# Five edits to a fused transform, mixing and two-layer kernel: where the first narrowing, an addition, a weight split, the threshold input and one transform stage stand

## The chip, the cores and the metric

The kernel runs on one core of a Trainium2 chip. A core has a matrix engine (TensorE, in the profile PE, with its weight loads as PEld), a vector engine (VectorE, DVE), an activation engine (ScalarE, ACT), a general engine (GpSimd, POOL) and a queue engine that issues DMAs (SyncE, SP; ACT issues the stores here). Each engine runs its own instructions in order. They meet through semaphores. The metric is the device time of one execution in microseconds (us), as the median of several runs.

## The reference, cut to what matters

The input `x` is 8 sequences of 3008 rows of 256 channels, all float32; the four matrices of the second part come in float64.

```
X = rfft(x, axis=1)                      # along the 3008 rows
Yr = Xr @ w_r - Xi @ w_i + b_r           # mixing over channels
Yi = Xr @ w_i + Xi @ w_r + b_i
Y = sign(Y) * max(|Y| - 0.01, 0)         # threshold, on both parts
a = irfft(Y, n=3008)
h = relu(a^T @ w_tok1) @ w_tok2          # over the rows (tokens), 256 wide
u = a + h^T
out = u + relu(u @ w_ch1) @ w_ch2        # over the channels, 1536 wide
```

## The kernel before

**Transform.** 3008 is 47 times 64. The forward transform is a 47-point stage (`dft47`, 13 groups of 5 positions; `stage1` multiplies a group by the constant `f1` and stores the result `a` to HBM as `a_d`), then a 64-point stage (`forward`: PSUM tile `px`, one step for each of 12 pairs `kp`). The inverse is again 64 points (`inverse`, tile `pi`, stored as `b_d`) and 47 points, the last one fused into the sum that makes `u` (`make_u`, tile `pu`, L738).

**Mixing and threshold.** `forward` copies `px` into `xf` as real and imaginary part (ACT, L442) and adds the two (L443), because the complex product is done with three real ones. `mix` runs three products into PSUM banks `p1` and `p2` (tile `pm`), adds the bias and the partial sums on DVE (L469 to L471), and thresholds the result. For the non-plain units the 32-bit operands are split into a high and a low part in the format fp32r (`split`, L137 on ACT for the high part, L140 for the low part), and each product is three matmuls (`mm3`, L178 to L180).

**Units.** The batch is worked in five units: sequence 0, sequence 1, and three pairs. Unit 0 is "plain" (unsplit float32 matmuls) and is done ahead of everything by `begin`; its 47-point result stays on the chip as `z`, is turned by PE (`turn`, tile `pz`) and copied to `a2` (tile `a`; the first two by DVE at L428, the others by ACT at L430).

**Work that `begin` carries as well.** The float64 matrices arrive as raw 64-bit words (`load_raw`) and are narrowed to float32 by two ACT and six DVE instructions (`narrow`, L151 to L158; tile `wide`). The 13 groups of `w_tok1` are narrowed and sent through the same 47-point stage (`prepare_w1`, tile `p`, L246 and L247, stored as `a_w`), read back (`load_w`, L319) and transformed over 64 points (`make_w`, tile `pw`, L327). `begin` loops over `n` from 0 to 21: `forward(n)`, `mix(n-1)`, one or two groups of `w_tok1`, `inverse(n-3)`; from n = NW = 10 on `make_w` and `tokens` (tile `gp`, L507). `prepare_mix` makes the sums of the mixing weights (L361 to L363), and `split_mix` splits them for the later units into `wmh` and `wml`, at n = 10.

**Main loop.** `channel(n)` does the two-layer part on up to 512 tokens (tiles `ph`, L178 to L180, and `po`; ACT L776 and DVE L777 between). Between its steps the loop at the end of the kernel runs the generator `spectral(u + 1)` of the next unit: each step yields an estimated cost, and a step runs while `left_s > pace * left_c`, that is, spread evenly over what is left of the present unit. A step that yields "wait" holds the generator until `left_c` has dropped by 10 more:

```
            if hold is not None:
                if left_c > hold:
                    continue
                pace, hold = left_s / left_c, None
```

**What sets the order.** The source is not the order of execution. The framework lays out each engine's instructions ahead of the run: it goes through the program with its own cost estimates, and gives an engine the earliest instruction of the source that it believes to be ready then. On the chip that order is kept, and an instruction whose data are late holds up all that are behind it on its engine. Transfers start when their buffer is free: five raw buffers, three `ld` tiles, two `ev` tiles (the `a` of `stage1`).

Lines that the prediction refers to: L137 and L140 (`split`), L151 to L158 (`narrow`), L167 (raw loads), L226 and L227 (`sum_diff`), L246 to L250 (`stage1`), L319, L327, L330 (`w_tok1`), L428 and L430, L440 to L443, L464 to L475 (`mix`).

Of the kernel before, what the change touches and what calls it, by code (L numbers as in the profile page):

```python
# [121 lines left out]
def tile_kernel(ctx: ExitStack, tc: tile.TileContext, io):  # L122
# [46 lines left out]

    def load_wide(src, n, pool=None, tag="o", raw=None):  # L170
        if raw is None:
            raw = load_raw(src, n, pool)
        rows = raw.shape[0]
        tmp = wk.tile([rows, 2, n], F32, tag=tag, name="wide", bufs={"o": 3, "hl": 4}[tag])
        return narrow(raw, tmp[:, 0], tmp[:, 1])

# [87 lines left out]

    def dft47(load, dst, w, ahead, eng, pool=None, turned=False):
        xs = [load(g) for g in range(ahead)]
        yield 0.0
        sds = {}

        def prepare(g):  # L270
            if g < NG:
                sds[g] = sum_diff(xs[g], g, w, eng, pool)
                xs[g] = None

        def divide(g):
            if g < NG and pool is None:
                sds[g] = split_x(sds[g], w)

        prepare(0)
        prepare(1)  # L280
        divide(0)
        for g in range(NG):
            if g + ahead < NG:
                xs.append(load(g + ahead))
            prepare(g + 2)
            divide(g + 1)
            if turned:
                stage1_turned(sds.pop(g), dst, g)
            else:
                stage1(sds.pop(g), dst, g, w, pool)  # L290
            yield 0.7 * w / C
# [12 lines left out]

    def prepare_w1(pool):
        def load(g):
            f = load_wide(None, 2 * DT, pool, ("hl", "o")[g % 7 % 2], raw=raws.pop(g)).rearrange("p (i w) -> p i w", i=2)
            load_raw1()
            return f

        return dft47(load, a_w, DT, 3, None, pool)
# [38 lines left out]
    def load_mix():  # L350
        wf = wc["wf2"] = const.tile([128, 2, 2, C], F32, tag="gl", name="wf2")
        for i, name in enumerate(("w_r", "w_i")):
            DMA.dma_start(out=wf[:, i], in_=io[name].rearrange("(t p) c -> p t c", p=128))
        load_raw1()
        for i, name in enumerate(("b_r", "b_i")):
            DMA.dma_start(out=bias[:, i], in_=io[name].rearrange("(o c) -> o c", o=1).to_broadcast([128, C]))
# [9 lines left out]

    def split_mix(y):
        for i, w in enumerate(wc["mix"]):
            V.tensor_copy(out=wmh[:1, i, 0, :1], in_=y[:1, 0, :1])
            split(wmh[:, i], wml[:, i], w, S, V)  # L370
# [21 lines left out]
    def parts(u):  # L392
# [40 lines left out]
        def forward(kp, b, a2):  # L433
            pt = bank("px")
            for t in range(2):
                for ab in range(2):
                    o = (2 * t + ab) * 128
                    cs = slice(t * 128, (t + 1) * 128)
                    x = a2[:, ab, b, cs]
                    PE.matmul(pt[:, o:o + 128], lhsT=x, rhs=f2cols(2 * kp + ab), start=True, stop=True)  # L440
            xf = wk.tile([128, 3, 4, 64], F32, tag="xth" if plain else "xf", name="xf", bufs=2)
            S.copy(out=xf[:, 1:3], in_=pt.rearrange("p (q i m) -> p i q m", i=2, m=64))  # L442
            (V if plain else G).tensor_tensor(out=xf[:, 0], in0=xf[:, 1], in1=xf[:, 2], op=ALU.add)  # L443
            if plain:
                return xf
            xh = wk.tile([128, 3, 2, 128], F32R, name="xth", bufs=2)
            xl = wk.tile([128, 3, 2, 128], F32R, name="xtl", bufs=2)
            fl = "p i (t a) m -> p i t (a m)"
            split(xh, xl, xf.rearrange(fl, t=2), S, V)
            return xh, xl  # L450

        def mix(kp, xt, yh, yl):
# [3 lines left out]
            else:  # L456
                p1, p2 = bank("pm1"), bank("pm2")
            for j, out in ((0, p1[:, :C]), (2, p2[:, C:]), (1, p2[:, :C])):

# [9 lines left out]
            V.tensor_tensor(out=y, in0=p1[:, :C].rearrange("p (o c) -> p o c", o=1).to_broadcast([128, 2, C]), in1=bias, op=ALU.add)  # L469
            V.tensor_tensor(out=y[:, 0], in0=p2[:, C:], in1=y[:, 0], op=ALU.add)  # L470
            V.tensor_tensor(out=y[:, 1], in0=p2[:, :C], in1=y[:, 1], op=ALU.add)  # L471
            if plain:
# [49 lines left out]
    def spectral(u):  # L522
        p = parts(u)
        nb = p.nb
        yield from dft47(p.load_unit, p.a, p.w, 3, V if u == 1 else G)
        yield "wait"
# [43 lines left out]
    def begin(sp):  # L570
# [14 lines left out]
        with tc.tile_pool(name="early", bufs=1) as early:  # L585
# [9 lines left out]
            load_mix()  # L595
            for _ in range(4):
                load_raw1()
# [3 lines left out]
            prepare_mix()  # L601
            w1 = prepare_w1(early)
            a2s = {0: p.turn(0), 1: p.turn(1)}
            next(w1)
            es, xts = {k: load_e(k) for k in range(2)}, {}
# [5 lines left out]
            for n in range(NW + KP):  # L611
                if n == NW:
                    split_mix(ys[NW - 2])
                if n < KP:
# [220 lines left out]
    for n, (u, at, cw) in enumerate(chunks):  # L835
# [8 lines left out]
        for c in channel(n):  # L844
# [9 lines left out]
            while left_s > pace * left_c:  # L854
                step = next(sp, None)
                if step is None:
                    left_s = -1e9
                elif step == "wait":
                    hold = left_c - 10.0
                    break  # L860
# [38 lines left out]
```

## Time and profile before

| | us |
|---|---|
| median of 3 runs | 2448.39 (2446.65 to 2452.34) |
| the profiled execution, own time | 2449.02 |
| its span, first to last instruction | 2447.0 |
| PE busy | 2423.0 (99% of the span) |
| DVE busy | 1109.7 (45%) |
| ACT busy | 876.4 (36%) |
| POOL busy | 305.7 (12%) |
| PE idle before its first matmul | 6.6 |
| last PE matmul to the end of the span | 4.3 |
| mean granted clock of TensorE | 0.998 |

Busy time is the time in which an engine executes instructions, the span the time from the first to the last instruction. The idle time of an engine stands with the engine whose result ended it. The granted clock is a share of full speed; here it takes one of two values, 1.00 or 0.50. The span less PE's busy time is 24.0 us, and 10.9 us of that are the start and the end of the program.

### The profile page before, as it was taken

The numbers are of one execution on the slowest core, as the hardware profiler recorded it, in microseconds if no ns is written. First come the engines' busy times: TensorE is split into PE (matmuls) and PEld (weight loads), VectorE is DVE, ScalarE is ACT, GpSimd is POOL, SyncE is SP. The second block draws the span as 40 slices with busy tenths as digits, with TensorE's granted clock in tenths as the row PEclk, the third lists the DMA queues.
The fourth block names the chain that finished last, engine by engine and source line by source line (L and its number), as shares of the span: only waits on it lengthen the run. The fifth ranks groups of instructions, "written<-read, shape, count | busy, mean of one in ns | idle before, by whom it ended". The sixth has DMA issues, their size and how long they took to land.

```text
span 2447.0 us, 31693 instructions
## 1 busy us (share of the span) xinstructions
PE 2423.0 (99%) x12848; PEld 2115.4 (86%) x12848; DVE 1109.7 (45%) x1774; ACT 876.4 (36%) x1580; POOL 305.7 (12%) x259
## 2 busy tenths in 40 slices
PE   8999999999999999999999999999999999999999
PEld 7778999988888888888888888888888888888887
DVE  7986655454455444433344363434334333232332
ACT  6764444443333343333333353333333222222222
POOL 0000222212223011111111120111111000000000
PEclk9999999999999999999999999999999999999999
DMA  7864335543324352222322263232321212112110
GB/s 206 254 211 144 101 115 154 162 142 99 94 84 129 107 176 79 61 80 87 93 75 68 89 182 100 77 99 76 93 67 37 70 50 63 56 52 81 37 56 18
DMA packets 144239, 246.07 MB, mean 101 GB/s; under 512 B 10653, under 2 KB 97917, under 8 KB 144093
## 3 DMA queue, kind: packets, MB, share of 16 engines
q1 hardware_dynamic: 114313, 190.56, 26.2%
q10 hardware_dynamic: 29780, 53.49, 7.0%
q8 instruction: 101, 1.65, 0.3%
q14 instruction: 45, 0.37, 0.0%
HBM read 159.73 MB, written 84.28 MB: 100 GB/s over the span
## 4 chain that ended last, share of the span: by engine, by line
PE 94%; DVE 2%; DMA 2%; ACT 1%; SPq 1%; issue 0%; POOL 0%; DVEq 0%; ACTq 0%; POOLq 0%
PE ph L178 10%; PE ph L179 10%; PE ph L180 10%; PE po L178 10%; PE po L180 10%; PE po L179 10%; PE pu L738 5%; PE px L440 3%; PE pm L178 2%; PE pm L180 2%; PE pm L179 2%; PE pu L178 2%; PE pu L179 2%; PE pu L180 2%; PE gp L178 2%; PE gp L179 2%
## 5 line engine op out<-in xcount | busy, mean ns | idle before, releaser
L777 DVE SCALAR_TENSOR_TENSOR hlo<-ph,hh 128x512 fp32r<-128x512 f32 (+4 forms) x588 | 391.9, 667 | 639.1 <-ACT hh L776 636.2
L776 ACT ACTIVATE hh<-ph 128x512 fp32r<-128x512 f32 (+4 forms) x588 | 340.7, 580 | 818.7 <-PE ph L180 816.6
L178 PE MATMUL ph<-uh,w 128*128 128x512 f32 (+4 forms) x1176 | 455.9, 388 | 1.0 <-DVE hlo L777 1.0
L179 PE MATMUL ph<-ul,w 128*128 128x512 f32 (+4 forms) x1176 | 449.6, 382 | 0.0
L178 PE MATMUL po<-hh,w2h 128*128 128x512 f32 (+4 forms) x1176 | 449.0, 382 | 0.0
L180 PE MATMUL ph<-uh,w 128*128 128x512 f32 (+4 forms) x1176 | 448.8, 382 | 0.0
L179 PE MATMUL po<-hlo,w2h 128*128 128x512 f32 (+4 forms) x1176 | 448.2, 381 | 0.0
L180 PE MATMUL po<-hh,w2l 128*128 128x512 f32 (+4 forms) x1176 | 448.1, 381 | 0.0
L180 PEld LDWEIGHTS ph<-uh,w 128*128 128x128 f32 x1176 | 221.1, 188 | 39.6
L179 PEld LDWEIGHTS po<-hlo,w2h 128*128 128x128 f32 x1176 | 221.1, 188 | 38.6 <-DVE hlo L777 0.2
L180 PEld LDWEIGHTS po<-hh,w2l 128*128 128x128 f32 x1176 | 221.0, 188 | 38.7
L178 PEld LDWEIGHTS po<-hh,w2h 128*128 128x128 f32 x1176 | 221.1, 188 | 38.6
L178 PEld LDWEIGHTS ph<-uh,w 128*128 128x128 f32 x1176 | 221.4, 188 | 36.3 <-DVE hlo L777 1.9
L179 PEld LDWEIGHTS ph<-ul,w 128*128 128x128 f32 x1176 | 221.5, 188 | 34.0 <-DVE ul L747 0.2
L140 DVE TENSOR_TENSOR xtl<-xf,xth 128x768 fp32r<-128x768 f32 x84 | 80.5, 959 | 207.3 <-ACT xth L137 207.3
L178 PE MATMUL pm<-wmh,xth 128*128 128x256 f32 x504 | 144.4, 287 | 1.1 <-ACT xth L137 1.1
L140 POOL TENSOR_TENSOR yl<-z,yh 128x512 fp32r<-128x512 f32 x72 | 92.8, 1289 | 412.8 <-ACT yh L137 412.8
L745 ACT COPY uf<-pu 128x470 f32<-128x470 f32 (+23 forms) x188 | 62.7, 376 | 227.5 <-PE pu L738 227.5
L180 PE MATMUL pm<-wmh,xtl 128*128 128x256 f32 x504 | 142.4, 283 | 0.0
L179 PE MATMUL pm<-wml,xth 128*128 128x256 f32 x504 | 142.4, 283 | 0.0
L738 PEld LDWEIGHTS pu<-g,b 96*128 96x128 f32 x1024 | 130.8, 191 | 3.4
L443 POOL TENSOR_TENSOR xf<-xf 128x256 f32<-128x256 f32 x84 | 69.2, 824 | 482.7 <-ACT xf L442 481.8
(126 smaller groups left out, 3230.1 us busy)
## 6 DMA issues: line engine op xcount, KB each, us to landing
wt<-wt_d SPq DMA_DIRECT2D x28, 940.0 KB, 5.7
x<-in_x SPq DMA_DIRECT2D x39, 480.0 KB, 4.4
a<-a_d SPq DMA_DIRECT2D x36, 512.0 KB, 3.9
b_d<-bt ACTq DMA_DIRECT2D x36, 512.0 KB, 3.3
out<-o SPq DMA_DIRECT2D x34, 512.0 KB, 2.8
a_d<-a ACTq DMA_DIRECT2D x36, 480.0 KB, 3.5
wt<-wt_d SPq DMA_DIRECT2D x21, 752.0 KB, 5.2
b<-b_d SPq DMA_DIRECT2D x32, 480.0 KB, 6.3
```

The source lines that it names most:

```text
L140: lo_eng.tensor_tensor(out=lo, in0=src, in1=hi.bitcast(F32), op=ALU.subtract)
L178: PE.matmul(out, lhsT=wh, rhs=xh, start=start, stop=False)
L179: PE.matmul(out, lhsT=wh, rhs=xl, start=False, stop=False)
L180: PE.matmul(out, lhsT=wl, rhs=xh, start=False, stop=stop)
L440: PE.matmul(pt[:, o:o + 128], lhsT=x, rhs=f2cols(2 * kp + ab), start=True, stop=True)
L443: (V if plain else G).tensor_tensor(out=xf[:, 0], in0=xf[:, 1], in1=xf[:, 2], op=ALU.add)
L738: PE.matmul(pt[:, s * TOKS:(s + 1) * TOKS], lhsT=b2[:, s, cs], rhs=g2[:, 0 if s0 + s == 0 else 1], start=False, stop=s == k - 1)
L745: S.copy(out=ufs[m][:, ct, lo - at:hi - at], in_=pt[:, lo - c0:hi - c0])
L776: S.activation(out=hh, in_=pt, func=AF.Relu)
L777: V.scalar_tensor_tensor(out=hlo, in0=pt, scalar=0.0, in1=hh.bitcast(F32), op0=ALU.max, op1=ALU.subtract)
```

## The change

Five edits. (1) The first of the 13 narrowings of `w_tok1` gets a one-row copy ahead of it that reads the second turned tile, so that it can't be ordered ahead of the copies of the first two turned tiles; one of the raw loads is issued ahead of the two bias loads, the number of loads staying five. (2) The addition of the two parts in `forward` runs on POOL for unit 0 too. (3) `split_mix` is called at n = 15, and its one-element copies (one for each of three weights) become one copy of three elements, which depends on the last mixed tile. (4) In `mix`, the two partial sums lie in `p2` in the order of the output, and one addition takes the place of two. (5) For units 2, 3 and 4 the 47-point stage yields "soon" after its first preparations, and is then held until `left_c` has dropped by 4.

```diff
--- before.py
+++ after.py
@@ -167,11 +167,13 @@
         DMA.dma_start(out=raw.rearrange("p n w -> p (n w)"), in_=src.bitcast(U32))
         return raw
 
-    def load_wide(src, n, pool=None, tag="o", raw=None):
+    def load_wide(src, n, pool=None, tag="o", raw=None, after=None):
         if raw is None:
             raw = load_raw(src, n, pool)
         rows = raw.shape[0]
         tmp = wk.tile([rows, 2, n], F32, tag=tag, name="wide", bufs={"o": 3, "hl": 4}[tag])
+        if after is not None:
+            V.tensor_copy(out=tmp[:1, :, 0], in_=after)
         return narrow(raw, tmp[:, 0], tmp[:, 1])
 
     def mm3(out, wh, wl, xh, xl, start, stop):
@@ -262,7 +264,7 @@
             in_=pt[:, :4 * GS * KH].rearrange("p (q n k) -> p q k n", q=4, n=GS)[:, :, :, :n],
         )
 
-    def dft47(load, dst, w, ahead, eng, pool=None, turned=False):
+    def dft47(load, dst, w, ahead, eng, pool=None, turned=False, lead=False):
         xs = [load(g) for g in range(ahead)]
         yield 0.0
         sds = {}
@@ -279,6 +281,8 @@
         prepare(0)
         prepare(1)
         divide(0)
+        if lead:
+            yield "soon"
         for g in range(NG):
             if g + ahead < NG:
                 xs.append(load(g + ahead))
@@ -302,9 +306,9 @@
         if n < NG:
             raws[n] = load_raw(io["wt1"][n], 2 * DT, wc["early"])
 
-    def prepare_w1(pool):
+    def prepare_w1(pool, after):
         def load(g):
-            f = load_wide(None, 2 * DT, pool, ("hl", "o")[g % 7 % 2], raw=raws.pop(g)).rearrange("p (i w) -> p i w", i=2)
+            f = load_wide(None, 2 * DT, pool, ("hl", "o")[g % 7 % 2], raw=raws.pop(g), after=None if g else after).rearrange("p (i w) -> p i w", i=2)
             load_raw1()
             return f
 
@@ -351,7 +355,8 @@
         wf = wc["wf2"] = const.tile([128, 2, 2, C], F32, tag="gl", name="wf2")
         for i, name in enumerate(("w_r", "w_i")):
             DMA.dma_start(out=wf[:, i], in_=io[name].rearrange("(t p) c -> p t c", p=128))
-        load_raw1()
+        for _ in range(2):
+            load_raw1()
         for i, name in enumerate(("b_r", "b_i")):
             DMA.dma_start(out=bias[:, i], in_=io[name].rearrange("(o c) -> o c", o=1).to_broadcast([128, C]))
 
@@ -365,8 +370,8 @@
 
 
     def split_mix(y):
+        V.tensor_copy(out=wmh[:1, :, 0, 0], in_=y[:1, 0, :3])
         for i, w in enumerate(wc["mix"]):
-            V.tensor_copy(out=wmh[:1, i, 0, :1], in_=y[:1, 0, :1])
             split(wmh[:, i], wml[:, i], w, S, V)
 
 
@@ -440,7 +445,7 @@
                     PE.matmul(pt[:, o:o + 128], lhsT=x, rhs=f2cols(2 * kp + ab), start=True, stop=True)
             xf = wk.tile([128, 3, 4, 64], F32, tag="xth" if plain else "xf", name="xf", bufs=2)
             S.copy(out=xf[:, 1:3], in_=pt.rearrange("p (q i m) -> p i q m", i=2, m=64))
-            (V if plain else G).tensor_tensor(out=xf[:, 0], in0=xf[:, 1], in1=xf[:, 2], op=ALU.add)
+            G.tensor_tensor(out=xf[:, 0], in0=xf[:, 1], in1=xf[:, 2], op=ALU.add)
             if plain:
                 return xf
             xh = wk.tile([128, 3, 2, 128], F32R, name="xth", bufs=2)
@@ -455,7 +460,7 @@
                 p1, p2 = pt[:, 0], pt[:, 1]
             else:
                 p1, p2 = bank("pm1"), bank("pm2")
-            for j, out in ((0, p1[:, :C]), (2, p2[:, C:]), (1, p2[:, :C])):
+            for j, out in ((0, p1[:, :C]), (2, p2[:, :C]), (1, p2[:, C:])):
 
                 wsel = {0: 0, 1: 2, 2: 1}[j]
                 for t in range(2):
@@ -467,8 +472,7 @@
             z = t4([128, 2, 2, C], "z")
             y, cl = z[:, 0], z[:, 1]
             V.tensor_tensor(out=y, in0=p1[:, :C].rearrange("p (o c) -> p o c", o=1).to_broadcast([128, 2, C]), in1=bias, op=ALU.add)
-            V.tensor_tensor(out=y[:, 0], in0=p2[:, C:], in1=y[:, 0], op=ALU.add)
-            V.tensor_tensor(out=y[:, 1], in0=p2[:, :C], in1=y[:, 1], op=ALU.add)
+            V.tensor_tensor(out=y, in0=p2.rearrange("p (i c) -> p i c", i=2), in1=y, op=ALU.add)
             if plain:
                 S.activation(out=cl, in_=y, func=AF.Relu, scale=-1.0, bias=lam)
                 S.activation(out=y, in_=y, func=AF.Relu, bias=lam)
@@ -522,7 +526,7 @@
     def spectral(u):
         p = parts(u)
         nb = p.nb
-        yield from dft47(p.load_unit, p.a, p.w, 3, V if u == 1 else G)
+        yield from dft47(p.load_unit, p.a, p.w, 3, V if u == 1 else G, lead=u > 1)
         yield "wait"
         steps = [(kp, b) for kp in range(KP) for b in range(nb)]
         a2s, ws, sts, xts, ys = {0: p.load_a(0)}, {}, {}, {}, {}
@@ -593,14 +597,14 @@
             next(x)
             DMA.dma_start(out=f2, in_=io["f2"])
             load_mix()
-            for _ in range(4):
+            for _ in range(3):
                 load_raw1()
             V.memset(lam, -LAM)
             for g in range(NG):
                 next(x)
             prepare_mix()
-            w1 = prepare_w1(early)
             a2s = {0: p.turn(0), 1: p.turn(1)}
+            w1 = prepare_w1(early, a2s[1][:1, 0, 0, :2])
             next(w1)
             es, xts = {k: load_e(k) for k in range(2)}, {}
             DMA.dma_start(out=sc, in_=io["scale"])
@@ -609,8 +613,8 @@
             held = [const.tile([128, KP // 2, 2, C], F32, tag=k, name="held") for k in ("w2h", "w2l")]
             ys = [held[k // 6][:, k % 6] for k in range(KP)]
             for n in range(NW + KP):
-                if n == NW:
-                    split_mix(ys[NW - 2])
+                if n == NW + 5:
+                    split_mix(ys[KP - 1])
                 if n < KP:
                     xts[n] = p.forward(n, 0, a2s.pop(n))
                     if n + 2 < KP:
@@ -855,8 +859,8 @@
                 step = next(sp, None)
                 if step is None:
                     left_s = -1e9
-                elif step == "wait":
-                    hold = left_c - 10.0
+                elif step in ("wait", "soon"):
+                    hold = left_c - (10.0 if step == "wait" else 4.0)
                     break
                 else:
                     left_s -= step
```

## Rows read from the trace of the kernel before

**Rows 1.** Waits of PE: line, waited for, us in total, times, longest us.

```profile
PE px L440 <- DVE a L428: 3.4, 1, 3.4
PE pm L464 <- DVE xf L443: 3.0, 1, 3.0
PE p L178 <- ACT a L248: 1.8, 1, 1.8
```

**Rows 2.** Stretches: us, busy by engine (instructions), granted clock, DMA share, GB/s.

```profile
24.00:26.00 2.00, 0.63 (x3) 0.63 (x4) 1.71 (x4) 0.82 (x2) 0.00 (x0) 0.50 0.97 246
...
30.00:32.00 2.00, 2.00 (x11) 1.83 (x10) 2.00 (x5) 1.76 (x5) 0.00 (x0) 0.80 0.99 270
...
498.00:502.00 4.00, 4.00 (x13) 3.52 (x12) 2.48 (x3) 3.80 (x6) 0.00 (x0) 0.57 0.59 153
```

**Rows 3.** Timeline of DVE, 20 to 48: start, us, line, operation, out and in, [idle before].

```profile
22.45 0.42 DVE L362 TENSOR_SCALAR wsum<-wsum 128x512 f32<-128x512 f32 x1
23.54 0.43 DVE L154 TENSOR_SCALAR wide<-raw 120x512 uint32<-120x512 uint32 x1 [0.67 <-DMA raw<-in_wt]
...
24.64 1.28 DVE L428 COPY a<-pz 128x512 f32<-128x512 f32 x2
...
26.49 0.43 DVE L154 TENSOR_SCALAR wide<-raw 120x512 uint32<-120x512 uint32 x1
...
28.84 0.68 DVE L158 TENSOR_TENSOR wide<-wide 120x512 f32<-120x512 f32 x1
...
36.59 0.69 DVE L469 TENSOR_TENSOR z<-pm,bias 128x512 f32<-128x512 f32 x1 [0.44 <-PE pm L464]
...
37.53 0.42 DVE L470 TENSOR_TENSOR z<-pm,z 128x256 f32<-128x256 f32 x1
```

**Rows 4.** Timeline of PE, 20 to 48, and from 92.

```profile
20.92 1.09 PE L425 MATMUL pz<-eye,z 128*128 128x128 f32 x8 [0.57 <-ACT z L260]
25.37 2.08 PE L440 MATMUL px<-f,a 128*128 128x128 f32 x8 [3.36 <-DVE a L428]
...
30.66 0.68 PE L246 MATMUL p<-wide,f 120*120 120x256 f32 x2
...
33.80 1.03 PE L464 MATMUL pm<-wf,xf 128*128 128x256 f32 x4
...
102.85 1.09 PE L327 MATMUL pw<-aw,fw 128*64 128x256 f32 x8
```

**Rows 5.** Additions of L443 on POOL: durations ns least/median/most, first and last start.

```profile
L443 POOL TENSOR_TENSOR xf<-xf x84: 734/738/1466, 228.8 to 1915.8; 128x256 f32<-128x256 f32 x84
```

**Rows 6.** Timeline of POOL and of DVE, 350 to 355.

```profile
350.56 3.17 POOL L140 TENSOR_TENSOR y<-z,y 128x512 fp32r<-128x512 f32 x1 [6.14 <-ACT y L137]
...
352.49 0.54 DVE L777 SCALAR_TENSOR_TENSOR hlo<-ph,hh 128x376 fp32r<-128x376 f32 x1
352.95 1.19 DVE L157 TENSOR_TENSOR wide<-raw,wide 128x376 f32<-128x376 f32 x1
```

**Rows 7.** Timeline of ACT, then of DVE, 84 to 126.

```profile
90.74 0.59 ACT L442 COPY xf<-px 128x512 f32<-128x512 f32 x1 [0.66 <-ACT bt L495]
...
95.31 0.58 ACT L248 COPY a<-p 120x512 f32<-120x512 f32 x1
...
118.05 0.84 ACT L330 ACTIVATE wf<-pw,sc 128x256 f32<-128x256 f32 x2 [2.18 <-PE pw L327]
...
100.41 0.40 DVE L443 TENSOR_TENSOR xf<-xf 128x256 f32<-128x256 f32 x1
```

**Rows 8.** Waits of the SP queue, 60 to 140.

```profile
SPq L319 <- DMA a_w<-a: 3.8, 1, 3.8
```

**Rows 9.** Timeline of ACT, then of SP, around 465 to 500.

```profile
496.81 1.07 ACT L248 COPY a<-p 120x512 f32<-120x512 f32 x2 [4.10 <-DMA a_d<-a]
...
465.26 18.49 SPq L410 DMA_DIRECT2D x<-in_x  x6
486.64 0.53 SPq L703 DMA_DIRECT2D wt<-wt_d  x1
```

## The prediction, made before the result was known

> **What bounds the kernel now.** I read the page first: PE is busy for 2423.0 of the 2447.0 us span, so the matrix engine bounds the kernel, and a change that leaves its matmuls as they are can win only from the 24.0 us in which it stands still and from stretches at its lower clock. Of the 24.0, 6.6 are the start and 4.3 the end, which no edit touches. Next the waits of PE, which say where the rest lies: 3.4 us in front of `px` behind the DVE copies, 3.0 in front of `pm` behind the addition L443, 1.8 in front of `p` behind an ACT copy [rows 1]. The timeline puts these at 22.0 to 25.4, 98.0 to 101.0 and 495.7 to 497.5. Then the stretches, for the clock: after the first of the three stops the granted clock is 0.50 (1.2 GHz instead of 2.4) and averages 0.80 over 30 to 32, so that it is back at 30.8; after the third it averages 0.57 over 498 to 502 [rows 2]; after the second it stayed at 1.00. PE works from 25.37 on, so the first low stretch costs half of 5.4 us, 2.7 us; the third costs 0.43 times 4.00, 1.7 us. All that these edits can aim at is therefore 3.4 + 2.7, 3.0, and 1.8 + 1.7: 12.6 us, 0.5% of the time. Between 510 and the end PE has practically no stop.
>
> **First narrowing behind the turned tiles.** PE ends the two turned tiles at 22.01 (20.92 + 1.09) [rows 4]. DVE ends the weight sums at 22.87, but its order has the first narrowing next, and L154 of it waits for a raw load until 23.54, so that the copies L428 come at 24.64 [rows 3] and `px` starts 0.73 later, at 25.37. With the narrowing behind them the copies can start at 22.87: 24.64 - 22.87 = 1.77 us sooner, `px` at 23.60, and a stop of 1.59 instead of 3.36. I expect the lower clock still to come, but for one stretch such as that of 498, where the stop before was 1.8 too: 1.7 lost instead of 2.7, another 1.0. So `px` and what follows could be 2.8 us ahead. What is late next is the narrowing itself: it starts at about 24.3 (both copies, 1.28, and the small copy) instead of 23.54, though without two copies in its midst. It ended at 29.52 (28.84 + 0.68) [rows 3], and PE took its result at 30.66 [rows 4]; if it again ends at 29.0 to 29.5, PE can be ahead only by some 1.2 to 1.7 us there. I take 1.5. Above: 4.5, if no low clock comes and PE's order puts other work there (1.77 + 2.7). Below: a loss of 1.0. Only group 0 is tied; if group 1's L154 slips into the freed place, the copies wait for its raw load, which landed at 26.49 [rows 3] and is now issued 1.2 us sooner: copies at 25.6, `px` at 26.4.
>
> From 31 to 98 PE has no stop to lose or give back. The other twelve groups are narrowed some us before PE takes them, so being 1.5 us ahead should last up to 98.
>
> **Parts' addition on POOL.** It takes 12 instructions of 0.42 us off DVE and puts 12 on POOL, 0.738 us each as a rule and 1.466 at most [rows 5]. In DVE's order the additions come late, behind narrowing: that of step 10 at 100.41, though ACT had its input ready at 91.33 (90.74 + 0.59) [rows 7]. On POOL it is done by 93 to 94, before PE gets there. The stop of 2.97 us before `pm` goes entirely. Next in PE's order is `pw`, at 102.85 without a stop [rows 4]. It needs the read-back L319, which waited 3.8 us for the last store of `a_w` to land [rows 8]; it can't have landed long before 102.85 itself. If PE comes to `pw` at 102.85 - 2.97 - 1.5 = 98.4, it waits for this chain: copy L248 at 95.31 [rows 7], store, read-back. L248 comes sooner with PE (1.5) and because DVE, which ACT waited for in this stretch, has less to do. I take 2.8 us sooner in all, so `pw` at about 100.0 and 2.8 us saved by both edits together, 1.3 of them by this one. Bounds: 0 (the store stays where it is) and 2.97.
>
> **Mixing split later.** Three ACT copies and three DVE subtractions leave the stretch 100 to 103, where they stand behind the addition, and come after 115, where ACT is idle for 2.18 us at a time [rows 7] and PE runs `pw` and `gp` two steps behind their inputs. That covers them: 0, and from -0.5 to +0.5 if the cover fails at one place. **Threshold input in one addition.** Two instructions of 0.42 become one as long as L469, 0.69 [rows 3]: 0.15 us less on DVE, 96 times. DVE isn't on the path after 101, and the wait for `pm` before it stays: 0, at best -0.5.
>
> **47-point work delayed.** It moves the first `stage1` of units 2 to 4 back by 5 to 7 us of channel work (the hold is looked at only once per step), not the first loads, which are issued ahead. For units 3 and 4 PE shows no stop at that stage, so nothing to gain. For unit 2 the stop at 495.7 comes from stores: ACT stood 4.10 us behind a store of `a` with two `a` buffers, while the next token weights (`wt`) and the last inputs arrived [rows 9]. Delaying the stage moves `x` loads, which run from 465 to 484 [rows 9], closer to the `wt` load at 486.6, without taking a byte away. I see nothing that removes the pile-up, so 0 for this edit; -3.5 (1.8 + 1.7) if the phase happens to suit, +10.5 if the stop occurs three times more.
>
> **Sum.** 2449.0 (the profiled execution's own time; 2.0 lie around its span) - 2.8 = 2446.2. The median of the runs shown is 0.6 below the profiled one, so 2445.6 for a median, 0.1% less than 2448.4.
>
> **A rule weighed.** The addition's price rests on POOL and DVE getting out of each other's way, and a row speaks against it: a POOL subtraction took 3.17 us from 350.56 on. It got nowhere while DVE ran narrowing without a break; it did its work from about 352.5 on, beside an L777 that reads PSUM, and the next DVE instruction, L157, then took 1.19 us, while L777 of the same width took 0.54 [rows 6]. The Trainium skill ("SBUF — State Buffer", "SBUF: two separate sides") calls the port pair of the two an exclusive lock: whoever starts first has it for a whole instruction, if the DVE one has two SBUF inputs or runs in a two-port mode. The trace agrees, and is harsher: POOL was passed over for several DVE instructions in a row. By that rule the sum would change at the first two additions alone, which is the second rival.
>
> **Rivals.** (a) More goes: the stop at 495 with its low clock goes too, or no low clock comes at 24. The first is worth 3.5 us, the second 1 to 3: 2448.4 - 2.8 - 3.5 = 2442. For it: the delay shifts which stores meet the `wt` load, and the first stop shrinks by half. Against: the low clock of 498 followed a stop no longer than the one that I expect at 22, and the bytes stay.
>
> (b) POOL is locked out at the start, so nothing is won. From the end of the copies to 36.15 DVE runs narrowing without a PSUM input, and has no idle time over 0.15 us (the 0.44 in front of L469 is the first) [rows 3]. The first addition, due at 26.3, would then run only when DVE stands at L469: at about 34.5, so that `pm` starts at 35.3 instead of 33.80 [rows 4], 1.5 us late, with another low stretch of 1.7. The 2.97 us at 98 would pay that back: 2448.4 - 2.97 + 1.5 + 1.7 = 2448.6. It decides if no gap lets POOL in before about 31. Tight gaps do exist, where DVE waits for ACT.
>
> (c) The change doesn't do what it says: group 1's narrowing takes the place of group 0's, the loss of 1.0 above, and the 1.3 to 2.3 gained at 98 to 101 remain: 2447.5.
>
> (d) Slower: the delayed stage of unit 2 meets the `wt` load with four `x` loads still to come, not one. Each puts a further store behind it, and each such stop costs 1.8 and 1.7 as the present one does: three more, +10.5, so 2448.4 - 2.8 + 10.5 = 2456.1. It decides from three `x` loads issued after `wt`. For it: the six loads of 465 to 484 come some 3 us apart, and the delay is 5 to 7. Against: by that spacing one or two move behind `wt`, hardly three, and the planner's order spreads the matmuls of `p` among those of `ph`.
>
> **How the numbers follow.** Chances: forecast 0.40, (a) 0.36, (b) and (c) 0.12 together, (d) 0.12. What a measurement can tell from no change is 0.2%, 4.9 us, so faster means under 2443.5. Forecast, (b) and (c) lie within it, (a) below it, (d) above 2453.3 but for a small part of it. Faster 0.37 (with the forecast's lower edge), same 0.52, slower 0.11. The forecast's own range is 2443.5 to 2447.5. Eight times in ten reaches from (a) with most of the low clock gone as well, 2439.5, to 2451.5, above (b); it leaves out (d) and the best of (a).
>
> **What would show it.** Step one right: the copies L428 follow L362 at once and `px` starts near 23.6; wrong, if an L154 stands between them. Step two: L443 on POOL under 1.5 us from step 3 on, no wait of `pm` near 98, and instead a PE wait at `pw` for a read-back of `a_w`, `pw` near 100. A wait of the first `pm` for POOL near 32 would be (b). Step five: the stop behind a store of `a`, in the waits of PE, near 500. I am wrong in the main if the time is under 2443, above all if that stop is gone, or if the granted clock never falls before 31.

## The result, and the profile after

The changed kernel takes 2455.9 us (median of 13 runs, 2453.67 to 2457.87), the kernel before 2449.6 beside it (13 runs): ratio 1.0024, 95% interval 1.0015 to 1.0032. It is slower by about 6 us, above the range of 2439.5 to 2451.5. The profiled execution took 2457.01, its span 2455.2 (before 2449.02 and 2447.0).

Busy time over the whole span, from the page:

```profile
PE 2424.3 (99%) x12848; PEld 2116.1 (86%) x12848; DVE 1098.7 (45%) x1665; ACT 875.3 (36%) x1580; POOL 333.4 (14%) x271
```

PE works 1.3 us longer than before (half clock) and stands still 6.9 longer. DVE got 11.0 cheaper; POOL got 27.7 dearer, where twelve additions of 0.738 come to 8.9. Line numbers shift: the addition L443 is L448 here, `pm` L464 is L469, `px` L440 is L445, the copies L428 are L433, `stage1`'s copy L248 is L250, and L176 is the new small copy. The waits of PE (line, waited for, total, times, longest):

```profile
PE pm L469 <- POOL xf L448: 8.2, 3, 7.1
...
PE ph L180 <- ACT a L250: 3.5, 1, 3.5
PE p L181 <- DVE xl L140: 2.0, 2, 1.6
...
PE px L445 <- DVE a L433: 0.5, 1, 0.5
```

Against [rows 1]: the 3.4 before `px` is down to 0.5, the wait of 3.0 at 98 is 0.88, but the first `pm` waits 7.1 for POOL, and the stop behind a copy of `a` at unit 2 is 3.5 instead of 1.8. The timeline of PE, which answers to [rows 4]:

```profile
22.21 1.09 PE L430 MATMUL pz<-eye,z 128*128 128x128 f32 x8 [0.57 <-ACT z L262]
23.77 1.16 PE L445 MATMUL px<-f,a 128*128 128x128 f32 x8 [0.47 <-DVE a L433]
...
33.81 2.08 PE L469 MATMUL pm<-wf,xf 128*128 128x256 f32 x4 [7.12 <-POOL xf L448]
...
39.37 0.60 PE L248 MATMUL p<-wide,f 120*120 120x256 f32 x2
...
106.72 1.09 PE L331 MATMUL pw<-aw,fw 128*64 128x256 f32 x8 [0.50 <-PE pm L469]
```

`pz` is 1.29 later than before. That part differs from execution to execution: e7 below, with the same first edit, has `pz` at 20.73, ahead of before. `px` is 1.60 ahead all the same, and `pw` 3.87 late (106.72 against 102.85). What DVE, ACT and POOL did meanwhile (three timelines; start, us, line, [idle before]):

```profile
23.03 1.28 DVE L433 COPY a<-pz 128x512 f32<-128x512 f32 x2
26.72 0.43 DVE L153 TENSOR_SCALAR wide<-wide 120x512 f32<-120x512 f32 x1 [2.41 <-ACT wide L151]
27.06 0.15 DVE L176 COPY wide<-a 1x2 f32<-1x2 f32 x1
27.13 0.74 DVE L154 TENSOR_SCALAR wide<-raw 120x512 uint32<-120x512 uint32 x2
27.80 0.67 DVE L155 SCALAR_TENSOR_TENSOR wide<-wide 120x512 uint32<-120x512 uint32 x1
...
32.16 0.67 DVE L158 TENSOR_TENSOR wide<-wide 120x512 f32<-120x512 f32 x1
32.76 0.41 DVE L154 TENSOR_SCALAR wide<-raw 120x512 uint32<-120x512 uint32 x1
```

```profile
26.00 0.68 ACT L151 ACTIVATE wide<-raw 120x512 f32<-120x512 f32 x1 [1.96 <-DMA raw<-in_wt]
```

```profile
27.80 6.64 POOL L448 TENSOR_TENSOR xf<-xf 128x256 f32<-128x256 f32 x2 [27.36 <-ACT xf L447]
```

The copies run at once, as forecast. But the next in DVE's order is the L153 of group 1, ahead of the small copy that opens group 0, and it waits 2.41 us for ACT's L151, which waits for raw load 1. (It can't be group 0's: the small copy writes into group 0's tile, and group 0's L151 and L153 come behind it.) Group 0 is narrowed at 32.83 (32.16 + 0.67), not at 29.52 [rows 3]. POOL's first addition stands from 27.80 and takes 5.96 us (the longest in the view of its line):

```profile
L448 POOL TENSOR_TENSOR xf<-xf x96: 719/738/5964, 27.8 to 1923.6; 128x256 f32<-128x256 f32 x96
```

It ends at 33.76, so, estimated with the median of 0.738, it began its work at 33.02: it was passed over for 5.2 us, in which DVE ran without a gap.

The price of the addition does not hold later either. From step 3 on seven of the nine additions took over 1.5 us, up to 3.76, where at most 1.466 was taken from [rows 5]. PE waited for two of them, 0.88 and 0.19.

Stretches that answer to [rows 2] (us, busy PE, PEld, DVE, ACT, POOL, granted clock, DMA share, GB/s):

```profile
30.20:37.00 6.80, 3.19 (x8) 2.57 (x9) 2.96 (x7) 4.29 (x8) 4.24 (x2) 0.50 0.90 205
...
488.00:496.00 8.00, 5.21 (x23) 3.90 (x22) 3.70 (x4) 1.68 (x3) 3.59 (x2) 1.00 1.03 305
497.80:504.60 6.80, 6.32 (x16) 4.65 (x15) 4.46 (x5) 4.26 (x9) 3.16 (x2) 0.50 0.75 215
```

And unit 2's 47-point stage, answering to [rows 9], first SP, then ACT:

```profile
476.57 3.53 SPq L415 DMA_DIRECT2D x<-in_x  x2
483.89 0.53 SPq L707 DMA_DIRECT2D wt<-wt_d  x1
...
487.25 14.27 SPq L415 DMA_DIRECT2D x<-in_x  x4
```

```profile
496.03 1.07 ACT L250 COPY a<-p 120x512 f32<-120x512 f32 x2 [6.35 <-DMA a_d<-a]
```

Before, six `x` loads ran ahead of `wt`; now two do, and four follow it. ACT stands 6.35 us behind a store instead of 4.10.

**The sum of the two profiles.** Up to 44: stops of 0.47 and 7.12, and half of 3.19 lost to the clock, make 9.2; before it was 3.36 and 2.7, 6.1. That is +3.1, and 1.29 of start: +4.4; at `pw` +3.87 stand. At unit 2 the stop grew by 1.7 and the low stretch from 3.4 to 6.8 us, another 1.7. Together 7.3 of the 8.2 by which the span grew. The 0.9 left lies in smaller stops; the largest new one, behind `xl` at 153.93, is 1.56 where before had 0.43. The own times differ by 8.0; without the start's 1.29 that is 6.7, near the 6.3 between the medians.

### The profile page after: what moved, and what is told of

Same layout as the page of the kernel before. It is cut to its first block, busy times and chain, and to the rows that moved or that the text cites. A ratio compares the mean times of both kernels' runs of the same rounds, so it can differ in the third digit from the quotient of the medians.

```text
span 2455.2 us, 31621 instructions
## 1 busy us (share of the span) xinstructions
PE 2424.3 (99%) x12848; PEld 2116.1 (86%) x12848; DVE 1098.7 (45%) x1665; ACT 875.3 (36%) x1580; POOL 333.4 (14%) x271
## 4 chain that ended last, share of the span: by engine, by line
PE 94%; DVE 3%; ACT 1%; DMA 1%; SPq 1%; POOL 1%; issue 0%; ACTq 0%; DVEq 0%; POOLq 0%
PE ph L180 10%; PE ph L181 10%; PE ph L182 10%; PE po L182 10%; PE po L180 10%; PE po L181 10%; PE pu L742 5%; PE px L445 3%; PE pm L180 2%; PE pm L182 2%; PE pm L181 2%; PE pu L180 2%; PE pu L181 2%; PE pu L182 2%; PE gp L180 2%; PE gp L181 2%
## 5 line engine op out<-in xcount | busy, mean ns | idle before, releaser
L448 POOL TENSOR_TENSOR xf<-xf 128x256 f32<-128x256 f32 x96 | 94.0, 979 | 554.5 <-ACT xf L447 554.5
```

Source lines behind the costliest of these rows:

```text
L448: G.tensor_tensor(out=xf[:, 0], in0=xf[:, 1], in1=xf[:, 2], op=ALU.add)
```

## The experiments

The theories, as the expectations name them. **L**: POOL is locked out at the start, and this is the loss. **O**: the narrowing comes too late, because group 1's L153 stands ahead of group 0 and waits for its raw load. **D**: the hold moves unit 2's loads onto the `wt` load. **P**: that pile-up is set by where earlier losses put it, not by the hold. "Ratio" is to the kernel before, of runs on the same chip, with its 95% interval. Edits 1 to 5 are numbered as in the change.

### The addition back on DVE: e1, and without the hold e4

```diff
-            G.tensor_tensor(out=xf[:, 0], in0=xf[:, 1], in1=xf[:, 2], op=ALU.add)
+            (V if plain else G).tensor_tensor(out=xf[:, 0], in0=xf[:, 1], in1=xf[:, 2], op=ALU.add)
```

> The changed kernel with unit 0's addition back on DVE, all else as changed. Theory L (the port lock is the cost at the start): the stop of 7.1 us in front of the first pm shrinks to 2 us or less, PE is 5 us further at the second group of w_tok1 (43.7 in the changed kernel), of which the stop near 98 takes back about 3: 2453 to 2454 us. Theory O (the narrowing itself comes too late, because group 1's L153 stands ahead of group 0's and DVE idles 2.4 us there): group 0 is narrowed no sooner than 31.5, so a PE stop of about 5 us between 26.7 and 32 stays, with the low clock behind it, and the stop near 98 comes on top: 2455 to 2458 us.

2462.74 us, ratio 1.0053 (1.0040 to 1.0066), above the ranges of both theories. With POOL out of the way the stop at the start stays, so L is not needed for it. Now PE comes to the narrowed weights first (PE, then DVE):

```profile
31.66 1.18 PE L248 MATMUL p<-wide,f 120*120 120x256 f32 x2 [5.66 <-DVE wide L158]
```

```profile
25.40 0.43 DVE L153 TENSOR_SCALAR wide<-wide 120x512 f32<-120x512 f32 x1 [1.79 <-ACT wide L151]
25.75 0.15 DVE L176 COPY wide<-a 1x2 f32<-1x2 f32 x1
...
29.30 0.67 DVE L158 TENSOR_TENSOR wide<-wide 120x512 f32<-120x512 f32 x1
...
30.84 0.67 DVE L158 TENSOR_TENSOR wide<-wide 120x512 f32<-120x512 f32 x1
```

The L158 that `p` waits for is the second one, behind that of the group whose L153 stands first: group 0 is overtaken. The time is that high for another reason as well: at 158.74 PE stops for 2.50 us behind ACT's `gh` (0.76 in before), and the granted clock is 0.50 from 156.9 to 170.5, with PE busy for 11.76 of it, which costs 5.9. What brings that stop about stays open.

> The changed kernel with the addition on DVE and without the hold; the first narrowing, the mixing split and the one addition stay as changed. L and D together: 2448 to 2450, not slower than the kernel before. O and D: 2451 to 2454, still slower than before, because the late narrowing alone stops PE for 5 us at 27 to 32. P: as e1 within 1.5 us.

2460.73, 1.0043 (1.0031 to 1.0056), above the ranges of L, O and D and 2.0 under e1: a stop of 4.4 at the same place, so it does not need the hold either. The stop behind `gh` is there too, 2.45.

### The change without the hold: e3

```diff
-        yield from dft47(p.load_unit, p.a, p.w, 3, V if u == 1 else G, lead=u > 1)
+        yield from dft47(p.load_unit, p.a, p.w, 3, V if u == 1 else G)
```

> The changed kernel without the hold of the 47-point stage in units 2 to 4, all else as changed. Theory D (the hold moves input loads and stores of unit 2 onto the wt load): the stop of 3.5 us near 493 becomes 1.8 and the low clock 3.4 us instead of 6.8, so 3.5 to 5 us less: 2451 to 2452.5. Rival P (the pile-up is set by where the 4 us lost at the start put the stage, not by the hold): a stop of 3 us or more stays near 490, time within 1.5 us of the changed kernel's 2455.9.

2453.31, 1.0018 (1.0009 to 1.0027), 2.6 less than the changed kernel, where D had 3.5 to 5. The six `x` loads run ahead of `wt` again, the stop at unit 2 is 1.4, and the first `pm` still waits 6.6 for POOL. D holds for a part; the larger part is ahead of it.

### One edit alone: e7 (1), e5 (2), e6 (5), e16 (3), e17 (4)

Each is the kernel before with that one edit's lines. Of each one line is shown, some of them cut short.

```diff
+            w1 = prepare_w1(early, a2s[1][:1, 0, 0, :2])        # e7, with its other lines
+            G.tensor_tensor(out=xf[:, 0], ...)                  # e5
+                    hold = left_c - (10.0 if step == "wait" else 4.0)   # e6
+                if n == NW + 5:                                 # e16
+            V.tensor_tensor(out=y, in0=p2.rearrange(...), in1=y, op=ALU.add)   # e17
```

> The kernel before with only the first narrowing put behind the turned tiles (and the raw load ahead of the bias loads). O: px starts 1.6 us sooner than before, but PE then stands 4 to 6 us for the first group of w_tok1 or the first pm, with a low clock, and the time is 2 to 4 us above before. L (this edit alone is harmless and worth what the prediction said): a stop of 2 us or less in front of p, 1 to 2.8 us faster than before.

2458.26, 1.0035 (1.0023 to 1.0048): edit 1 alone costs some 8.7 us, more than twice what O had. DVE shows the same order and wait:

```profile
26.34 0.43 DVE L153 TENSOR_SCALAR wide<-wide 120x512 f32<-120x512 f32 x1 [2.08 <-ACT wide L151]
26.68 0.15 DVE L176 COPY wide<-a 1x2 f32<-1x2 f32 x1
```

PE stands 4.3 us in front of `p`. The rest of the loss is at step 10, where the addition is still on DVE and the stop grows from 2.97 to 4.60; behind it the granted clock is 0.50 for 6.6 us (106.1 to 112.7):

```profile
107.12 2.04 PE L467 MATMUL pm<-wf,xf 128*128 128x256 f32 x4 [4.60 <-DVE xf L446]
```

> The kernel before with only unit 0's addition on POOL. Theory L (POOL gets nowhere while DVE runs narrowing without a break): the first addition, due at about 28.3, ends no sooner than 34, PE stands 4 us or more in front of the first pm, most of it paid back at 98 to 101, where the stop of 3.0 shrinks below 1.5: 2450 to 2453 us, no faster than before. Theory O (the loss of the change is the late narrowing, and POOL's addition alone is a gain): the stop at the first pm stays under 2 us and the time is 2 to 3 us under before, 2446.5 to 2448.

2446.24, 0.9985 (0.9976 to 0.9994): faster than both kernels, by 3.3 against before. POOL, DVE and PE:

```profile
28.29 1.14 POOL L443 TENSOR_TENSOR xf<-xf 128x256 f32<-128x256 f32 x1 [27.85 <-ACT xf L442]
```

```profile
28.16 0.68 DVE L155 SCALAR_TENSOR_TENSOR wide<-wide 120x512 uint32<-120x512 uint32 x1
28.76 1.22 DVE L158 TENSOR_TENSOR wide<-wide 120x512 f32<-120x512 f32 x1
```

```profile
100.08 1.09 PE L327 MATMUL pw<-aw,fw 128*64 128x256 f32 x8 [1.06 <-DMA aw<-a_w]
```

POOL gets in between two DVE instructions, and the next takes 1.22 instead of 0.68 [rows 3]. The stop at 98 is gone, and `pw` starts at 100.08 behind the read-back: both as the prediction had it. But six of the nine additions from step 3 on took 1.67 to 3.56, against the "under 1.5" that was to show the step right.

> The kernel before with only the hold of the 47-point stage in units 2 to 4. Theory D (the hold itself brings the inputs and stores of unit 2 onto the wt load): the stop near 497 grows from 1.8 to 3 or more and the low clock behind it from 3.4 to 6.8 us: 2452 to 2454.5. Rival P (the stop depends on where earlier losses have put the stage, not on the hold): within 1.5 us of before.

2451.06, 1.0010 (1.0001 to 1.0019): the hold alone costs 1.5. Its SP row and ACT row:

```profile
482.04 14.24 SPq L412 DMA_DIRECT2D x<-in_x  x4
```

```profile
490.76 1.07 ACT L248 COPY a<-p 120x512 f32<-120x512 f32 x2 [6.30 <-DMA a_d<-a]
```

No loss stands ahead of unit 2 here, and still four loads come behind `wt` (478.66) and the stop is 3.43: D, not P. The low clock behind it lasts 3.4 us, as before, not 6.8, and the time is lower than D's range.

> The kernel before with edit 3 alone (split of the mixing weights at step 15, one three-element copy). My prediction cost it at nothing (-0.5 to +0.5). Theory O+D (edits 1 and 5 are the whole loss): 2449 to 2450 us, ratio 0.9995 to 1.0005, every stop of PE as before, the 98 stop 2.5 to 3.0 since the addition is still on DVE. Rival (edit 3 changes the planner's order in the stretch 100 to 125 and brings a stop of its own there): 2451 or more, with a new PE stop between 100 and 130.

2450.42, 1.0003 (0.9994 to 1.0012).

> The kernel before with edit 4 alone (two partial sums in one addition). My prediction cost it at nothing, at best -0.5. Theory O+D: 2449 to 2450 us, ratio 0.9995 to 1.0005, every stop of PE as before. Rival (the shorter DVE work lets the planner reorder the rest, so that a stop moves): a difference of 1.5 us or more in either sign, to be seen in the waits of PE.

2449.68, 1.0004 (0.9995 to 1.0013). Neither can be told from nothing. In e17 one stop moved: 1.55 behind the low part `xl` near 147, where before had 0.43; there a POOL subtraction and DVE's L158 (1.66 instead of 0.68) met. The stop at 98 shrank to 1.1 in return.

### Edit 1 with three groups tied: e14 (edit 1 alone), e20 (with 2), e19 (the whole change), e21 (without the hold)

```diff
-after=None if g else after
+after=after if g < 3 else None
```

> The kernel before with the first three narrowings put behind the turned tiles, not the first alone. O (in the change, group 1's L153 stands ahead of group 0's small copy and waits for its raw load until 26): DVE starts group 0 by 24.5, narrows it by 30, PE stands 2.5 us or less in front of p, and the time is 4 us or more under that of the single tie (2458.3). If the tie itself is what costs (any start of the narrowing behind the copies is too late): PE stands 4 us or more in front of p and the time is within 3 us of the single tie.

2449.93, 1.0004 (0.9995 to 1.0014): 8.3 less than e7, by two more small copies. DVE:

```profile
22.48 1.28 DVE L431 COPY a<-pz 128x512 f32<-128x512 f32 x2
23.79 0.30 DVE L176 COPY wide<-a 1x2 f32<-1x2 f32 x3
24.01 0.41 DVE L154 TENSOR_SCALAR wide<-raw 120x512 uint32<-120x512 uint32 x1
...
29.77 0.69 DVE L158 TENSOR_TENSOR wide<-wide 120x512 f32<-120x512 f32 x1
```

With group 1 unable to go ahead, DVE starts group 0 at 24.01 and has it at 30.46, 2 us sooner than e7 (32.45). In the time this is O. One of its signs failed: the stop in front of `p` is no shorter than in e7, since PE came to it 2 us sooner too:

```profile
30.60 1.13 PE L248 MATMUL p<-wide,f 120*120 120x256 f32 x2 [4.46 <-DVE wide L158]
```

The step-10 stop is 1.05 instead of 4.60. The raw load moved ahead of the bias loads is in e14 as in e7, so it isn't the loss. But the repaired edit gains nothing over before either: what PE no longer waits for at `px` it waits for at `p`.

> The kernel before with edits 1 and 2, the first three narrowings tied, and nothing of edits 3, 4 and 5. If the parts add up: tie of three (+0.4) and addition on POOL (-3.3), so 2446 to 2447, and at best 2444.5 if the earlier px is kept. Theory L: POOL is locked out at the start once the narrowings stand in one block behind the copies, the first pm waits for it until about 33, and the time is 2449 or more.

2447.69, 0.9992 (0.9984 to 1.0001); POOL's first addition took 1.00 us. No better than e5.

> The changed kernel with all of the first three narrowings tied behind the turned tiles, not group 0's alone. Theory O (edit 1 loses because group 1's narrowing stands ahead of group 0's and waits for its raw load): group 0 narrowed by about 29.5, the 12 groups of w_tok1 no longer 4.5 us late, 2448.5 to 2449.5 us, that is about 7 less than the changed kernel; the hold's 1.5 to 2.5 stay. Theory L (port lock at the start is the loss): the first addition on POOL still enters when DVE's narrowing ends near 33, the first pm waits for it, and the time stays at 2454 to 2456.

2451.76, 1.0013 (1.0004 to 1.0022): 4.1 less than the change, not the 7 expected. POOL's first addition took 0.99 and `pm` waited at most 2.3, so the lock went with the order. What is left over before is the hold, as the next run shows.

> The changed kernel with three narrowings tied and without the hold. Theory O+D (the two causes add): tying three gave -4.1 and leaving out the hold -2.6, so 2455.9 - 6.7 = 2449.2, no different from before. Rival (the two overlap, since each moves the same low clock near 500 or the same later phases): 2450.5 to 2452, no lower than the better of the two alone.

2448.39, 0.9998 (0.9989 to 1.0007). With both causes mended the loss is gone.

**The start in all traces.** From the first `pz` to the `pi` ahead of the step-10 stop PE took 76.0 us before (20.92 to 96.96) and 79.2 in the change (22.21 to 101.45):

```profile
96.96 1.03 PE L492 MATMUL pi<-held,ef 128*128 128x256 f32 x4
```

```profile
101.45 1.03 PE L496 MATMUL pi<-held,ef 128*128 128x256 f32 x4
```

The same stretch in the other runs, one execution each:

| narrowing | unit 0's addition on DVE | on POOL |
|---|---|---|
| not tied | before 76.0, e6 75.5, e16 74.9, e17 75.6, e22 74.6 | e5 75.6, e18 76.7, e23 75.7, e24 73.8, e25 76.1 |
| group 0 alone tied | e1 80.0, e4 80.4, e7 80.8 | the change 79.2, e3 79.1 |
| three groups tied | e14 77.9 | e19 75.0, e20 76.4, e21 74.9 |

(e11, with both engines, took 75.6.) The five kernels with group 0 alone tied are the five slowest, whichever engine adds. That is O. The stretch is no shorter with the addition on DVE, so the wait of POOL adds nothing to it that can be seen here.

### Edits 2 to 5 and 2 to 4: e23, e18; and their parts e24, e25, e11

e18 is the kernel before with edits 2, 3 and 4; e23 adds the hold; e24 has 2 and 3, e25 2 and 4; e11 is e18 with the first two additions on DVE:

```diff
+            (V if plain and kp < 2 else G).tensor_tensor(out=xf[:, 0], ...)
```

> The changed kernel without edit 1: edits 2 to 5 remain. If the parts add: 2449.5 - 3.3 (addition) + 1.0 and 0.3 (split, one addition, both measured as nothing) + 1.5 (hold) = 2449 at most, 2447.7 with the two at 0; theory O is then the whole of the step from before to after. Theory L (the POOL addition at the start is the loss whatever the narrowing): the first addition enters near 33 and the time is 2452 or more. Rival (planner's order moves with each edit, parts don't add): any other time, with a stop of PE at another place than 22 to 35, 98 to 101 and 495.

2452.45, 1.0014 (1.0005 to 1.0023); the waits of PE:

```profile
PE ph L178 <- ACT a L248: 3.6, 1, 3.6
...
PE p L179 <- DVE xl L140: 1.6, 1, 1.6
```

3.4 less than the whole change, so edit 1 is about half of the loss, and L fails again: POOL's first addition took 1.12. But 2452.45 is more than I expected of the parts, and the stop behind `xl` is at another place than those named: that was the rival's sign.

> The kernel before with edits 2, 3 and 4 (POOL addition, split later, one addition), without edits 1 and 5; that is the kernel of e23 without the hold. If edits 3 and 4 are worth nothing beside the addition too: 2446 to 2447 (-3.3 against before), and the hold then costs e23 some 6. If edits 3 and 4 take the addition's gain back, and the hold costs the 1.5 to 2.6 measured elsewhere: 2449.5 to 2451, with a stop of 1.5 behind the low part xl near 147 as in e23.

2448.81, 0.9997 (0.9988 to 1.0006), between the two ranges. The hold therefore costs e23 3.6.

> Edits 2 and 3 alone. If edit 3 takes the addition's gain back: 2448.5 to 2450, with a new stop of PE between 100 and 150. If it is worth nothing: 2446 to 2447.

2448.40, 0.9999 (0.9990 to 1.0008).

> Edits 2 and 4 alone. If edit 4 takes the addition's gain back (the stop of 1.5 behind xl near 147 was also in edit 4 alone): 2448.5 to 2450, with that stop. If it is worth nothing: 2446 to 2447.

2448.31, 0.9993 (0.9984 to 1.0002). With edit 3 or 4 beside it the addition measures 0.9 to 1.0 less than before, not 3.3. In e18 and e24 the stop behind `xl` near 147 is 1.6 (0.35 in e5), in e25 1.05. That could be what takes the gain, but the intervals of the four kernels overlap, so this stays open.

> The kernel before with the addition on POOL from step 2 on (the first two stay on DVE), the mixing split at n = 15 and the one addition; neither the tied narrowing nor the hold. O and L both: the first 31 us are as before, the stop of 3.0 at 98 goes to 1 or less, and 1 to 3 us are won: 2446.5 to 2448.5. If the POOL additions cost DVE as much as they free, the stop at 98 stays above 2 and the time is within 1 us of before.

2452.26, 1.0013 (1.0004 to 1.0021): a miss. The step-10 stop stays at 2.4, now behind POOL, and keeping two additions on DVE is worse than none.

### The hold on units 3 and 4 alone: e22

```diff
-lead=u > 1)
+lead=u > 2)
```

> The kernel before with the hold for units 3 and 4 alone. Theory D (the hold costs by moving unit 2's x loads onto the wt load near 485): unit 2's stop is as before (1.8 near 496), 2449 to 2450, ratio 0.999 to 1.001. Rival (the hold costs in units 3 and 4 as well): the loss of 1.5 us of the hold alone stays at 1 or more.

2448.33, 0.9998 (0.9989 to 1.0007). SP issues the six loads ahead of `wt` again, and the stop is 1.4:

```profile
464.95 19.07 SPq L412 DMA_DIRECT2D x<-in_x  x6
486.34 0.54 SPq L705 DMA_DIRECT2D wt<-wt_d  x1
```

The hold's cost is at unit 2 and its `wt` load.

### Both causes in one table

Medians in us; all rows have edits 2, 3 and 4.

| | no hold | hold | the hold's cost |
|---|---|---|---|
| without edit 1 | 2448.81 (e18) | 2452.45 (e23) | 3.6 |
| edit 1 as changed | 2453.31 (e3) | 2455.9 (the change) | 2.6 |
| three groups tied | 2448.39 (e21) | 2451.76 (e19) | 3.4 |
| cost of group 0 alone tied | 4.5 | 3.5 | |

The kernel before, run beside each, had 2449.1 to 2449.6. Taken each without the other, the two causes cost 4.5 and 3.6, 8.1 in all; together they cost 7.1 (2455.9 less 2448.81). The intervals reach some 2 us either way, so 1.0 can't be told from nothing, and the two add as far as can be seen. Edits 2 to 4 give back 0.5 (2449.27 before beside e18, less 2448.81).

## Why the prediction was wrong, step by step

**First narrowing: the step that failed.** Right were the copies at once behind the weight sums and `px` near 23.6 (23.77). Wrong was "if it again ends at 29.0 to 29.5": it ended at 32.83. I asked only whether group 1 could slip ahead of the copies, and rival (c) priced that at 1.0. (The 26.49 that it takes for the landing of group 1's raw load is only when DVE came to it: the row has no idle time [rows 3].) It slipped one place later, between the copies and the small copy, where DVE has 2.41 us of nothing to do until raw load 1 has landed. The tie holds back group 0 and nothing else, so the planner had an instruction free that it believed ready. The cost is 3.5 to 4.5 in this company and 8.7 alone, where -1.5 was forecast; alone it is larger because the addition left on DVE then stops PE for 4.60 at step 10.

**The addition on POOL: outcome right, two steps of the reasoning wrong, and its value only alone.** e5 has -3.3 measured against -1.3 for this edit and -2.8 with edit 1; the stop at 98 went, and `pw` came to wait for the read-back. But the 91.33 [rows 7] at which the prediction took the input of step 10 to be ready belongs to the addition that DVE did at 93.67. The copy for step 10 is the next L442 (before, then e5):

```profile
98.44 0.59 ACT L442 COPY xf<-px 128x512 f32<-128x512 f32 x1
```

```profile
95.04 0.59 ACT L442 COPY xf<-px 128x512 f32<-128x512 f32 x1
```

Before, it ends at 99.03, so POOL could have had the sum at 99.8 at the soonest (an estimate with 0.738), and about two thirds of the 2.97 would have stayed. The stop went because ACT's copy came 3.40 us sooner as well. DVE was then 3.8 us further (L469 at 90.82 instead of 94.61), having done ten additions fewer; that this moved the copy was not tried. That the whole stop went is so far luck. The second wrong step is the price of the addition, at most 1.466: it took up to 3.56 in e5 and up to 5.96 in the change. In the change the stop at 98 shrank too, but PE came there 4.5 us late.

**Rival (b)** came to pass in one place only: behind the late narrowing, POOL's first addition began at 33.02 (34.5 forecast). The Trainium skill ("SBUF — State Buffer", "SBUF: two separate sides") has the loser of the shared port pair block for the whole instruction of the other. The trace agrees in kind: in e5 DVE's next instruction took 0.54 longer once POOL was in. It differs in length, since POOL lost to DVE from 27.80 to 33.02. In the change and in e3 the lock is the form that the stop takes; e1 and e7 have the loss without it, and with three groups tied it is gone. By the table of the start it adds nothing that can be seen: with the addition on DVE the stretch is as long.

**Split later and one addition**: 0, and 0 measured within 0.13% either way. That DVE isn't on the path after 101 did not hold: in e17 PE stops behind its `xl` near 147.

**The delayed 47-point work: the second failed step**, put at 0, costs 1.5 alone and 2.6 to 3.6 with the others. "One or two move behind `wt`, hardly three": four did. Rival (d) had the mechanism and its deciding point (three loads behind `wt`), with a chance of 0.12; its price was wrong. It is one stop of 3.5 instead of 1.8, with up to 3.4 us more at half clock, not three further stops. The price of +10.5 was three to four times too high for this company. That its 2456.1 is so near the measured 2455.9 is luck: about half of that loss is the narrowing's.

## What to carry to other kernels

A dependence added to hold one instruction back leaves the next free ones where they were: look at what the planner will put into the freed place, and tie every instruction that could wait there for a transfer. Delaying an early stage moves its loads as well; count how many pass the next large load before calling the delay free. Edits to one crowded start should be timed one by one: here the lowest median is that of a single edit of the five, 2446.24 us.

## What the runs showed of the hardware that was not expected

POOL's addition of 0.738 us (the median), the first of unit 0, took 1.14 in e5 and 5.96 in the change, both times while DVE ran narrowing without a gap. In the eleven traces with unit 0's additions on POOL, 63 of these took over 1.3 us. In 57 of the 63 the last 0.738, the time in which POOL is estimated to have worked, overlaps a mixing sum on DVE, which has `pm` in PSUM as an input. That points to these sums as the place where POOL gets in; no run tried it. In the change, for instance (POOL, then DVE):

```profile
49.14 3.76 POOL L448 TENSOR_TENSOR xf<-xf 128x256 f32<-128x256 f32 x1 [4.54 <-ACT xf L447]
```

```profile
52.23 0.69 DVE L474 TENSOR_TENSOR z<-pm,bias 128x512 f32<-128x512 f32 x1
```

The 5.96 ended as DVE ran out of work (it then stood for 5.11 us). What let POOL in sooner in e5, beside an L158, was not found. When it does get in beside narrowing, DVE pays: L158 took 1.22 and, near 147 in e17, 1.66, against 0.68.

The lower clock after unit 2's stop does not follow from the length of the stop alone: before, it came after a stop of 1.77 (0.57 over 498 to 502, [rows 2]); in e20, after one of the same 1.77, it did not.

```profile
495.18 0.50 PE L180 MATMUL p<-xh,f1r 120*120 120x512 f32 x1 [1.77 <-ACT a L250]
```

```profile
494.00:498.00 4.00, 2.82 (x13) 2.53 (x14) 1.47 (x2) 3.45 (x7) 0.49 (x1) 1.00 0.43 113
498.00:502.00 4.00, 4.00 (x20) 3.40 (x20) 2.23 (x3) 2.64 (x5) 0.00 (x0) 1.00 0.70 194
```
